# A causal convolution and a gated two-layer product on one core: channels in three chunks of 64, and the convolution a tile ahead

## The chip, the cores and the metric

The kernel runs on one core of a Trainium2 chip. The core has five engines with queues of their own: TensorE (PE in the profile, its weight loads PEld), VectorE (DVE), ScalarE (ACT), GpSimd (POOL) and SyncE (SP), whose queue issues most DMAs here. The metric is the device time of one execution, in microseconds (us); less is better.

## The reference

The input x has 8 sequences of 4096 tokens with 192 channels. Each of 8 heads (24 channels) has 7 weights, which a softmax turns into a causal filter over the tokens. The result, 32768 rows of 192, goes through a product with `w_in` (192 x 2048), the function h cos(h), and a product with `w_out` (2048 x 192).

```python
out = np.einsum('hk,bskhg->bshg', softmax(weight), x_unf)   # 7 taps, causal, zeros ahead of a sequence
h = out.reshape(B * S, D) @ w_in
g = h * np.cos(h)
return (g @ w_out).astype(np.float32)
```

## The kernel before

Tokens go in 64 tiles of 512 (index `t`), two of them a unit of 1024 (index `u`). The 2048 columns of `w_in` go in 8 pairs of 128 (index `j`); the work for one tile and one pair is called a slot here. In slot (t, j) TensorE computes product 1 (h, two PSUM banks, one for each of the pair's two blocks i), ScalarE the sine of h + pi/2, VectorE their product g in bf16. In the same slot TensorE runs an eighth of product 2 of the tile before, `mm2(t - 1, j)`: 16 matmuls of 192 columns. So g of a tile is made in one tile's slots and used in those of the next, and in slot 7 ScalarE copies the finished output from PSUM to SBUF (`o_sb`), which a later DMA stores.

All these matmuls use half of TensorE's rows (64 of 128); one on the upper and one on the lower half run at the same time, as long as they write different PSUM banks. Where the halves change banks, a `Turn` orders them: the last matmuls before the change mark a no-operation on SP's queue, and the first ones after it wait for that.

```python
def mark(self, *insts):
    self.nop = nc.sync.nop()
```

The convolution multiplies the tokens of a unit by banded 128 x 128 matrices, heads 4c to 4c + 3 in `conv_part(u, c)`: 12 matmuls of 192 columns, two halves of six with a Turn between them; ScalarE casts the result to bf16 into `ct`. `double_unit` (GpSimd) copies the upper 64 channels beside themselves, since 192 = 128 + 64 and product 1 takes the 64 on either row half. `turn_unit` transposes ct to cT (channels on partitions) by a DMA from SP. All of unit u + 1 is prepared in the two tiles of unit u: part 0 in slot 0 of the even tile, part 1 in slot 0 of the odd one, and there doubling in slot 0 and the transpose in slot 3.

Product 1 of a slot (class `Hidden`) is six half-row matmuls of 512 columns. `first` puts the upper half on bank 0 and the lower on bank 1 (two pairs), `last` the lower on bank 0 and the upper on bank 1 (one pair), with a Turn between them and product 2 in between to pass its time. Tile 0 has no product 2 and uses `full`, with 128-row matmuls in part.

The PSUM has 8 banks: three buffers of two banks for h (`h_pool`, taken in turn by product 1 and by the convolution's parts), one of two for the output (`o_ps`). An h buffer is free again when VectorE has made its product (or ScalarE has cast a convolution part). Each engine works through its instructions in the order in which the code writes them (`manual_schedule`).

Of the kernel before, what the change touches and what calls it, by code (L numbers as in the profile page):

```python
# [16 lines left out]
def kernel(  # L17
# [8 lines left out]
    nc = tc.nc  # L26
# [15 lines left out]
    C2 = D - 128  # L42
# [63 lines left out]
    w1 = consts.tile([128, Dff], BF16)  # L106
    w2 = consts.tile([128, NP, 128], BF16)
# [36 lines left out]
    def conv_part(u, c):  # L144
# [4 lines left out]

        def mm(i, k, start=False):  # L150
# [4 lines left out]
                out=ps[:, i // 2, (i % 2) * UB * G : (i % 2 + 1) * UB * G].rearrange("p (n g) -> p n g", g=G),  # L155
                lhsT=band[rows, h, 128 if prev else 0 : 256 if prev else 128],
                rhs=xb[rows, 0 if prev else 1 : UB if prev else UB + 1, h * G : (h + 1) * G],
# [6 lines left out]
        mm(3, 2)  # L164
        turn = Turn()
        turn.mark(up, mm(3, 1))
# [6 lines left out]
        mm(3, 0)  # L173
        if c == 0:
            ct_tiles[u] = ct_pool.tile([128, UB, 256], BF16, name="ct")
        o = ct_tiles[u][:, :, 4 * c * G : (4 * c + 4) * G].rearrange("p n (b i g) -> p b i n g", b=2, i=2)
        for b in range(2):
            nc.scalar.copy(o[:, b], ps[:, b, 0 : 2 * UB * G].rearrange("p (i n g) -> p i n g", i=2, n=UB))  # L178
# [4 lines left out]
    def double_unit(u):  # L183
        ct = ct_tiles[u]
        nc.gpsimd.tensor_copy(out=ct[:, :, D:256], in_=ct[:, :, 128:D])  # L185

    def turn_unit(u):
        ct = ct_tiles.pop(u)
        t = cT_pool.tile([128, UB, 2, 128], BF16, name="cT")
        nc.sync.dma_start_transpose(out=t.rearrange("p n c k -> p (n c) k"), in_=ct.rearrange("p n k -> p (n k)"))  # L190
        cT[u] = t
        cT.pop(u - 2, None)

    def conv_unit(u):
        for c in range(2):
            list(conv_part(u, c))
        double_unit(u)
        turn_unit(u)

    cast_unit(0)  # L200
    nc.gpsimd.tensor_copy(out=w2, in_=w2_f)  # L201
    nc.vector.tensor_copy(out=w1, in_=w1_f)  # L202
    conv_unit(0)
# [8 lines left out]
    class Hidden:  # L212


        def __init__(self, t, j):
            self.t, self.j = t, j
            self.c = cT[t // TPU]
            self.n0 = (t % TPU) * NB
            self.h = h_pool.tile([128, 2, T], FP32, name="h")

        def part(self, i, rows, w, c, start=False, stop=False):
            return nc.tensor.matmul(out=self.h[:, i, :], lhsT=w, rhs=self.c[rows, self.n0 : self.n0 + NB, c, :],  # L222
                             start=start, stop=stop)

        def w1(self, i, rows):
            f = 2 * self.j + i
            return w1[rows, f * 128 : (f + 1) * 128]

        def full(self):
            for i in range(2):  # L230
                r = slice(64 * i, 64 * i + 64)
                self.part(i, r, w2[r, self.j, :], 1, start=True)
            for i in range(2):
                self.part(i, slice(0, 128), self.w1(i, slice(0, 128)), 0, stop=True)

        def first(self):

            up, lo = slice(0, 64), slice(64, 128)
            self.part(0, up, self.w1(0, up), 0, start=True)
# [118 lines left out]
```

## Time and profile before

| | |
|---|---|
| median of 3 runs | 891.72 us (890.39 to 892.23) |
| the profiled execution | 885.45 us, its span from first to last instruction 883.7 us |
| busy in the span: TensorE, VectorE, ScalarE, GpSimd | 85%, 71%, 70%, 9% |
| mean granted clock of TensorE | 0.996 of full speed |
| starts of the output copies of tiles 1 and 63 | 57.67 and 872.33 us |

The profile is of one execution. Busy time is the time in which an engine has an instruction under way; on TensorE matmuls overlap, so their own durations add up to more than they cost. How long a piece of work takes TensorE is read from the distance of starts.

### The profile page before, as it was taken

The numbers are of one execution on the slowest core, as the hardware profiler recorded it, in microseconds if no ns is written. First come the engines' busy times: TensorE is split into PE (matmuls) and PEld (weight loads), VectorE is DVE, ScalarE is ACT, GpSimd is POOL, SyncE is SP. The second block draws the span as 40 slices with busy tenths as digits, with TensorE's granted clock in tenths as the row PEclk, the third lists the DMA queues.
The fourth block names the chain that finished last, engine by engine and source line by source line (L and its number), as shares of the span: only waits on it lengthen the run. The fifth ranks groups of instructions, "written<-read, shape, count | busy, mean of one in ns | idle before, by whom it ended". The sixth has DMA issues, their size and how long they took to land.

```text
span 883.7 us, 26935 instructions
## 1 busy us (share of the span) xinstructions
PE 751.2 (85%) x12016; PEld 535.3 (61%) x12016; DVE 631.0 (71%) x524; ACT 620.6 (70%) x707; POOL 76.3 (9%) x101
## 2 busy tenths in 40 slices
PE   0588989888889888889898898988888988889897
PEld 0166666666666566566666666666666665666665
DVE  1377777777777777777777777777777776767785
ACT  0477777777777777677777777777777766767775
POOL 1111110011111011110001111001111001110000
PEclk9999999999999999999999999999999999999999
DMA  8133332233332133332233332223333223332121
GB/s 238 24 79 80 98 88 71 55 97 89 87 97 72 46 94 94 83 97 72 49 93 93 83 97 74 70 70 98 79 96 94 58 62 97 80 96 73 44 61 56
DMA packets 138084, 72.52 MB, mean 82 GB/s; under 512 B 68200, under 2 KB 137840, under 8 KB 137840
## 3 DMA queue, kind: packets, MB, share of 16 engines
q1 hardware_dynamic: 136896, 70.27, 29.9%
q8 instruction: 94, 1.54, 0.7%
q10 hardware_dynamic: 1072, 0.53, 0.2%
q14 instruction: 22, 0.18, 0.1%
HBM read 28.84 MB, written 25.17 MB: 61 GB/s over the span
## 4 chain that ended last, share of the span: by engine, by line
issue 82%; POOL 8%; PE 6%; DMA 2%; ACT 1%; DVE 1%; SPq 0%; POOLq 0%; ACTq 0%
POOL x_bf L138 5%; PE o_ps L274 3%; PE h L222 2%; POOL ct L185 2%; DMA skew<-row_d 1%; POOL x_bf L137 1%; DMA row_d<-row 1%; DVE g L255 1%; PE h L154 0%; SPq L190 0%; ACT o_sb L284 0%; ACT cs L252 0%; POOL x_bf L135 0%; DMA w_sb<-in_weight_dram 0%; ACT L90 0%
## 5 line engine op out<-in xcount | busy, mean ns | idle before, releaser
L255 DVE TENSOR_TENSOR g<-h,cs 128x1024 bf16<-128x1024 f32 x512 | 626.2, 1224 | 225.8 <-ACT cs L252 200.5
L252 ACT ACTIVATE cs<-h 128x1024 bf16<-128x1024 f32 x512 | 525.2, 1026 | 176.5 <-PE h L222 176.4
L222 PE MATMUL h<-cT,w 64*128 64x512 bf16 x3056 | 520.0, 378 | 76.6 <-SPq L118 42.7
L274 PE MATMUL o_ps<-wo,g 64*128 64x192 bf16 x8192 | 514.5, 243 | 2.1 <-ACT o_sb L284 1.8
L274 PEld LDWEIGHTS <-g 64*128 64x128 bf16 x8192 | 395.6, 94 | 145.6 <-SPq L118 10.1
L222 PEld LDWEIGHTS <-w 64*128 64x128 bf16 x3056 | 160.0, 94 | 105.0 <-issue 55.1
L154 PE MATMUL h<-x_bf,band 64*128 64x192 bf16 x768 | 66.1, 250 | 49.3 <-DVE g L255 28.8
L154 PEld LDWEIGHTS <-band 64*128 64x128 bf16 x768 | 39.3, 95 | 93.2 <-DVE g L255 29.0
L178 ACT CAST ct<-h 128x384 bf16<-128x384 f32 x128 | 55.0, 482 | 47.2 <-PE h L154 37.4
L185 POOL COPY ct<-ct 128x512 bf16<-128x512 bf16 x32 | 19.6, 614 | 672.4 <-ACT ct L178 672.4
L284 ACT COPY o_sb<-o_ps 128x768 f32<-128x768 f32 x64 | 51.1, 798 | 33.6 <-PE o_ps L274 33.6
L138 POOL CAST x_bf<-x_f 128x1536 bf16<-128x1536 f32 x32 | 46.9, 1466 | 86.4 <-DMA x_f<-in_x_dram 86.4
L104 DVE COPY band<-skew 128x2048 bf16<-128x2048 bf16 x1 | 0.7, 695 | 15.2 <-DMA skew<-row_d 15.2
L137 POOL COPY x_bf<-x_bf 128x192 bf16<-128x192 bf16 x24 | 8.3, 347 | 0.0
L90 ACT ACT_TABLE_LOAD x1 | 1.3, 1283 | 2.2 <-DMA w_sb<-in_weight_dram 2.2
L135 POOL MEMSET x_bf<- 128x192 bf16 x8 | 2.1, 257 | 0.3 <-POOLq L342 0.3
L206 DVE CAST wo<-wo_f 128x768 bf16<-128x768 f32 x4 | 2.0, 555 | 0.0
L201 POOL CAST w<-w_f 128x1024 bf16<-128x1024 f32 x1 | 1.0, 1040 | 4.2 <-DMA w_f<-in_moe_w_in_dram 4.2
L252 ACT ACT_TABLE_LOAD x1 | 1.3, 1283 | 0.0
L202 DVE CAST w<-w_f 128x2048 bf16<-128x2048 f32 x1 | 1.2, 1221 | 0.0
L92 DVE TENSOR_REDUCE wsum<-wexp 8x1 f32<-8x7 f32 x1 | 0.1, 148 | 1.3 <-ACT wexp L90 1.3
L85 DVE MEMSET row<- 8x256 uint32 x1 | 0.3, 272 | 0.8 <-PEq L342 0.8
(9 smaller groups left out, 1.4 us busy)
## 6 DMA issues: line engine op xcount, KB each, us to landing
x_f<-in_x_dram SPq DMA_DIRECT2D x32, 768.0 KB, 4.8
out_dram<-o_sb SPq DMA_DIRECT2D x64, 384.0 KB, 2.6
wo_f<-in_moe_w_out_dram SPq DMA_DIRECT2D x1, 1536.0 KB, 13.2
w_f<-in_moe_w_in_dram SPq DMA_DIRECT2D x1, 1024.0 KB, 7.7
w_f<-in_moe_w_in_dram SPq DMA_DIRECT2D x2, 256.0 KB, 8.4
skew<-row_d ACTq DMA_DIRECT2D x1, 512.0 KB, 9.3
cT<-ct SPq DMA_TRANSPOSE x32, 4.3
w_sb<-in_weight_dram ACTq DMA_DIRECT2D x1, 0.2 KB
```

Of the source, the lines that this page charges most:

```text
L135: nc.gpsimd.memset(xb[:, 0, :], 0.0)
L137: nc.gpsimd.tensor_copy(out=xb[:, 0, :], in_=bf[u - 1][:, UB, :])
L138: nc.gpsimd.tensor_copy(out=xb[:, 1 : UB + 1, :], in_=xt)
L154: return nc.tensor.matmul(out=ps[:, i // 2, (i % 2) * UB * G : (i % 2 + 1) * UB * G].rearrange("p (n g) -> p n g", g=G), lhsT=band[rows, h ...
L178: nc.scalar.copy(o[:, b], ps[:, b, 0 : 2 * UB * G].rearrange("p (i n g) -> p i n g", i=2, n=UB))
L185: nc.gpsimd.tensor_copy(out=ct[:, :, D:256], in_=ct[:, :, 128:D])
L206: nc.vector.tensor_copy(out=wo[:, 4 * q : 4 * q + 4, :], in_=wo_f[:, 4 * q : 4 * q + 4, :])
L222: return nc.tensor.matmul(out=self.h[:, i, :], lhsT=w, rhs=self.c[rows, self.n0 : self.n0 + NB, c, :], start=start, stop=stop)
L252: nc.scalar.activation(out=cs, in_=self.h, func=AF.Sin, bias=math.pi / 2.0, scale=1.0)
L255: nc.vector.tensor_tensor(out=g_tiles[self.t][:, 2 * self.j : 2 * self.j + 2, :], in0=self.h, in1=cs, op=ALU.mult)
L274: m = nc.tensor.matmul(out=ps[:, b, si * D : (si + 1) * D], lhsT=g[rows, f, s * 128 : (s + 1) * 128], rhs=wo[rows, f, :], start=(swap == 0 ...
L284: nc.scalar.copy(sb.rearrange("p (b s) d -> p b (s d)", b=2), ps[:, :, 0 : 2 * D])
```

## The change

The 192 channels are cut into three chunks of 64 (`NC = 3`), eight channels of every head in each (`R = 8`), and every chunk is doubled. The weights of product 1 are loaded in the same cut, block i of a pair on row half i. So a slot's product 1 is three pairs; the upper row half writes bank 0 and the lower one bank 1 all the time, and no Turn is needed. The six matmuls stand ahead of all 16 of product 2, and the sine and product are issued there.

Part 0 of a unit's convolution is computed a tile earlier, in the odd tile two units before; part 1 in the even tile of the unit before, with the doubling in slot 0 and the transpose in slot 4 of that tile. In slot 0 the first half of a convolution part now stands ahead of product 1, the second half behind it, and the two casts are issued behind the slot's sine. The cast of x stands in slot 4 and its load in slot 6 of even tiles. Of the start, unit 1's part 0 and unit 2's load now stand ahead of the loop.

```diff
-    w1_f = consts.tile([128, Dff], FP32)
-    w2_f = consts.tile([128, NP, 128], FP32)
-    w2_src = moe_w_in[128:D, :].rearrange("c (j t f) -> t c j f", t=2, f=128)
-    nc.sync.dma_start(out=w1_f, in_=moe_w_in[0:128, :])
-    for t in range(2):
-        nc.sync.dma_start(out=w2_f[t * 64 : t * 64 + 64, :, :], in_=w2_src[t])
+    w_f = consts.tile([128, NC, NP, 128], FP32)
+    w_src = moe_w_in.rearrange("(h k r) (j t f) -> k t h r j f", h=H, r=R, t=2, f=128)
+    for k in range(NC):
+        for t in range(2):
+            nc.sync.dma_start(out=w_f[64 * t : 64 * t + 64, k, :, :], in_=w_src[k, t])
...
+        pv = ps[:, :, 0 : UB * 2 * G].rearrange("p b (n k i r) -> p b i n k r", n=UB, k=NC, i=2)
...
-                out=ps[:, i // 2, (i % 2) * UB * G : (i % 2 + 1) * UB * G].rearrange("p (n g) -> p n g", g=G),
+                out=pv[:, i // 2, i % 2],
...
         mm(3, 0)
+        yield
         if c == 0:
-            ct_tiles[u] = ct_pool.tile([128, UB, 256], BF16, name="ct")
+            ct_tiles[u] = ct_pool.tile([128, UB, NC, 2, 64], BF16, name="ct")
...
-        nc.gpsimd.tensor_copy(out=ct[:, :, D:256], in_=ct[:, :, 128:D])
+        nc.gpsimd.tensor_copy(out=ct[:, :, :, 1, :], in_=ct[:, :, :, 0, :])
...
-        t = cT_pool.tile([128, UB, 2, 128], BF16, name="cT")
+        t = cT_pool.tile([128, UB, NC, 128], BF16, name="cT")
...
+    load_unit(2)
+    list(conv_part(1, 0))
...
+    def mm1(t, j):
+        c = cT[t // TPU]
+        n0 = (t % TPU) * NB
+        h = h_pool.tile([128, 2, T], FP32, name="h")
+        for k in range(NC):
             for i in range(2):
...
+                rows = slice(64 * i, 64 * i + 64)
+                nc.tensor.matmul(out=h[:, i, :], lhsT=w[rows, k, j, :], rhs=c[rows, n0 : n0 + NB, k, :],
+                                 start=(k == 0), stop=(k == NC - 1))
+        cs = cos_pool.tile([128, 2, T], BF16, name="cs")
+        nc.scalar.activation(out=cs, in_=h, func=AF.Sin, bias=math.pi / 2.0, scale=1.0)
...
+        nc.vector.tensor_tensor(out=g_tiles[t][:, 2 * j : 2 * j + 2, :], in0=h, in1=cs, op=ALU.mult)
...
     for t in range(NT + 1):
-        u_next = t // TPU + 1
+        u, second = divmod(t, TPU)
+        cu, cc = (u + 2, 0) if second else (u + 1, 1)
         for j in range(NP):
...
+            conv = conv_part(cu, cc) if j == 0 and cu < NU else iter(())
+            next(conv, None)
+            if t < NT:
+                mm1(t, j)
+            next(conv, None)
+            next(conv, None)
+            if t > 0:
                 mm2(t - 1, j, 0, 8)
...
+            if j == 0 and second == 0 and cu < NU:
+                double_unit(cu)
+            if j == 4 and second == 0 and cu < NU:
+                turn_unit(cu)
+            if j == 4 and second == 0 and u + 2 < NU:
+                cast_unit(u + 2)
+            if j == 6 and second == 0 and u + 3 < NU:
+                load_unit(u + 3)
```

What this does to the order is shown at three places. The lines of the changed kernel are: L156 the convolution's matmul (before L154), L182 its cast (L178), L225 product 1 (L222), L228 the sine (L252), L249 product 2 (L274), L259 the output copy (L284). A number behind a name tells buffers apart, and `waits` names the engine whose semaphore an instruction waits for.

TensorE in an ordinary slot of tile 3 before, from the last pair of product 1 of one slot (h_871) to product 2 of the next (h_901):

```order
L222 LDWEIGHTS w1_120 [waits SP_sequencer_49]
L222 MATMUL h_871<-cT_384,w1_120 128x512
...
L274 LDWEIGHTS g_543
L274 MATMUL o_ps_761<-wo_122,g_543 128x192
...
L222 LDWEIGHTS w1_120
L222 MATMUL h_901<-cT_384,w1_120 128x512 [waits DVE_49]
...
L222 LDWEIGHTS w2_121
L222 MATMUL h_901<-cT_384,w2_121 128x512
...
L274 LDWEIGHTS g_543
L274 MATMUL o_ps_761<-wo_122,g_543 128x192
```

And now, from the end of one slot's product 2 to the product 2 behind the next slot's product 1:

```order
L249 LDWEIGHTS g_543
L249 MATMUL o_ps_792<-wo_123,g_543 128x192
L225 LDWEIGHTS w_122
L225 MATMUL h_890<-cT_259,w_122 128x512 [waits DVE_49]
...
L225 LDWEIGHTS w_122
L225 MATMUL h_890<-cT_259,w_122 128x512
...
L249 LDWEIGHTS g_543
L249 MATMUL o_ps_792<-wo_123,g_543 128x192
```

The six matmuls of product 1 (six weight loads, six matmuls; the first and the last shown) stand together, and the wait for SP's queue within product 1 is gone.

TensorE in slot 0 of tile 4 before: `first` of product 1 (h_983), the convolution's first half (h_989), `last`, the second half, product 2:

```order
L222 LDWEIGHTS w1_120 [waits DMAHW7_49]
L222 MATMUL h_983<-cT_869,w1_120 128x512 [waits DVE_49]
...
L154 LDWEIGHTS band_118 [waits DVE_49]
L154 MATMUL h_989<-x_bf_898,band_118 128x192 [waits Pool_49]
...
L222 LDWEIGHTS w1_120 [waits SP_sequencer_49]
L222 MATMUL h_983<-cT_869,w1_120 128x512
...
L154 LDWEIGHTS band_118 [waits SP_sequencer_49]
L154 MATMUL h_989<-x_bf_898,band_118 128x192
...
L274 LDWEIGHTS g_781
L274 MATMUL o_ps_1008<-wo_122,g_781 128x192 [waits Activation_49]
```

And now the convolution's first half (h_995), product 1 (h_1003), the second half, product 2:

```order
L156 LDWEIGHTS band_120
L156 MATMUL h_995<-x_bf_680,band_120 128x24x8 [waits DVE_49]
...
L225 LDWEIGHTS w_122 [waits DMAHW1_49]
L225 MATMUL h_1003<-cT_678,w_122 128x512 [waits DVE_49]
...
L156 LDWEIGHTS band_120 [waits SP_sequencer_49]
L156 MATMUL h_995<-x_bf_680,band_120 128x24x8
...
L249 LDWEIGHTS g_781
L249 MATMUL o_ps_1022<-wo_123,g_781 128x192 [waits Activation_49]
```

The convolution takes its h buffer ahead of product 1 of slot 0 instead of behind it, and product 1 is one piece between its halves.

ScalarE around the end of tile 1 before: the sine of slot 6, the output copy, the sine of slot 7, the casts of a convolution part, the sines of slots 0 and 1 of tile 2:

```order
L252 ACTIVATE cs_467<-h_443 128x1024 [waits DVE_49,PE_49]
L284 COPY o_sb_278<-o_ps_277 128x768 [waits PE_49]
L252 ACTIVATE cs_495<-h_470 128x1024 [waits DVE_49]
L178 CAST ct_520<-h_504 128x2x8x24 [waits DMAHW1_49,PE_49,Pool_49]
L178 CAST ct_520<-h_504 128x2x8x24
L252 ACTIVATE cs_541<-h_498 128x1024 [waits DVE_49]
L252 ACTIVATE cs_569<-h_545 128x1024 [waits DVE_49,PE_49]
```

And now, at the end of the same tile: the sine of slot 7, the output copy, the sine of slot 0, the casts, the sine of slot 1:

```order
L228 ACTIVATE cs_506<-h_499 128x1024 [waits DVE_49,PE_49]
L259 COPY o_sb_325<-o_ps_324 128x768 [waits PE_49]
L228 ACTIVATE cs_541<-h_534 128x1024 [waits DVE_49,PE_49]
L182 CAST ct_321<-h_526 128x24x16 [waits PE_49]
L182 CAST ct_321<-h_526 128x24x16
L228 ACTIVATE cs_579<-h_572 128x1024 [waits DVE_49,PE_49]
```

The sine of slot 7 stands ahead of the output copy and the sine of slot 0 ahead of the casts.

## Rows read from the trace of the kernel before

**Rows 1.** page, part 1: busy us (share) x instructions of each engine
```profile
PE 751.2 (85%) x12016; PEld 535.3 (61%) x12016; DVE 631.0 (71%) x524; ACT 620.6 (70%) x707; POOL 76.3 (9%) x101
```

**Rows 2.** page, part 5: groups | busy us, mean ns | idle before
```profile
L255 DVE TENSOR_TENSOR g<-h,cs 128x1024 bf16<-128x1024 f32 x512 | 626.2, 1224 | 225.8 <-ACT cs L252 200.5
...
L222 PE MATMUL h<-cT,w 64*128 64x512 bf16 x3056 | 520.0, 378 | 76.6 <-SPq L118 42.7
L274 PE MATMUL o_ps<-wo,g 64*128 64x192 bf16 x8192 | 514.5, 243 | 2.1 <-ACT o_sb L284 1.8
...
L154 PE MATMUL h<-x_bf,band 64*128 64x192 bf16 x768 | 66.1, 250 | 49.3 <-DVE g L255 28.8
```

**Rows 3.** timeline, one ordinary slot: start us, us, engine, line, operation, xcount [idle]
```profile
405.80 0.61 PE L222 MATMUL h<-cT,w 64*128 64x512 bf16 x4
...
406.23 0.68 PE L274 MATMUL o_ps<-wo,g 64*128 64x192 bf16 x12
...
406.72 0.40 PE L222 MATMUL h<-cT,w 64*128 64x512 bf16 x2
...
406.94 0.35 PE L274 MATMUL o_ps<-wo,g 64*128 64x192 bf16 x4
...
407.10 0.61 PE L222 MATMUL h<-cT,w 64*128 64x512 bf16 x4
407.15 1.02 ACT L252 ACTIVATE cs<-h 128x1024 bf16<-128x1024 f32 x1 [0.28 <-PE h L222]
```

**Rows 4.** timeline, the boundary from tile 28 to tile 29
```profile
412.33 0.61 PE L222 MATMUL h<-cT,w 64*128 64x512 bf16 x4
412.55 0.80 ACT L284 COPY o_sb<-o_ps 128x768 f32<-128x768 f32 x1 [0.45 <-PE o_ps L274]
...
413.24 1.03 ACT L252 ACTIVATE cs<-h 128x1024 bf16<-128x1024 f32 x1
413.41 0.34 PE L154 MATMUL h<-x_bf,band 64*128 64x192 bf16 x4 [0.47 <-DVE g L255]
...
414.31 1.23 DVE L255 TENSOR_TENSOR g<-h,cs 128x1024 bf16<-128x1024 f32 x1 [0.95 <-ACT cs L252]
414.56 0.86 ACT L178 CAST ct<-h 128x384 bf16<-128x384 f32 x2 [0.28 <-PE h L154]
...
415.58 0.61 PE L222 MATMUL h<-cT,w 64*128 64x512 bf16 x4 [0.41 <-DVE g L255]
```

**Rows 5.** timeline of ScalarE: output copies of tiles 1, 2, 61 and 63
```profile
57.67 0.80 ACT L284 COPY o_sb<-o_ps 128x768 f32<-128x768 f32 x1 [0.45 <-PE o_ps L274]
...
70.07 0.80 ACT L284 COPY o_sb<-o_ps 128x768 f32<-128x768 f32 x1 [0.45 <-PE o_ps L274]
...
850.14 0.80 ACT L284 COPY o_sb<-o_ps 128x768 f32<-128x768 f32 x1 [0.45 <-PE o_ps L274]
...
872.33 0.80 ACT L284 COPY o_sb<-o_ps 128x768 f32<-128x768 f32 x1 [0.45 <-PE o_ps L274]
```

**Rows 6.** timeline, the issue of a transpose on SP's queue, in an odd tile
```profile
419.85 1.72 SPq L190 DMA_TRANSPOSE cT<-ct  x1
...
421.68 0.39 PE L222 MATMUL h<-cT,w 64*128 64x512 bf16 x2 [1.07 <-SPq L118]
```

**Rows 7.** view of tile ct: durations ns min/median/max, last row us to landing
```profile
L185 POOL COPY ct<-ct x32: 613/614/615, 24.6 to 839.3; 128x512 bf16<-128x512 bf16 x32
L190 SPq DMA_TRANSPOSE cT<-ct x32: 1327/1920/3107, 25.2 to 843.8; - x32
...
DMA to landing us min/median/max: 4.3/4.3/5.0
```

**Rows 8.** timeline of the start: first product 1, first sines
```profile
29.67 1.58 PE L222 MATMUL h<-cT,w 64*128 64x512 bf16 x4 [6.06 <-DMA cT<-ct]
...
35.12 2.86 ACT L252 ACTIVATE cs<-h 128x1024 bf16<-128x1024 f32 x3
```

**Rows 9.** timeline of ScalarE: the last output copy
```profile
879.32 0.80 ACT L284 COPY o_sb<-o_ps 128x768 f32<-128x768 f32 x1 [5.27 <-PE o_ps L274]
```

More of the change, by code (lines that the diff above doesn't have):

```diff
@@ L41 @@
     NP = NF // 2
-    C2 = D - 128
+    NC = D // 64
+    R = G // NC
     xf = x.rearrange("b s d -> (b s) d")
@@ L104 @@
     nc.vector.tensor_copy(out=band, in_=skew[:, :, ::-1])
-    w1 = consts.tile([128, Dff], BF16)
-    w2 = consts.tile([128, NP, 128], BF16)
+    w = consts.tile([128, NC, NP, 128], BF16)
     wo = consts.tile([128, NF, D], BF16)
@@ L163, in conv_part @@
         mm(2, 2)
-        mm(3, 2)
+        mm(3, 1)
         turn = Turn()
-        turn.mark(up, mm(3, 1))
+        turn.mark(up, mm(3, 2))
         yield
@@ L210 @@
     o_state = {}
[L212 to L229, printed above, removed]
-            for i in range(2):
[L231 to L239, printed above, removed]
-            self.part(1, lo, self.w1(1, lo), 0, start=True)
-            self.turn = Turn()
-            self.turn.mark(self.part(0, up, w2[up, self.j, :], 1), self.part(1, lo, w2[lo, self.j, :], 1))
-        def last(self):
-            up, lo = slice(0, 64), slice(64, 128)
-            self.turn.wait(self.part(1, up, self.w1(1, up), 0, stop=True),
-                           self.part(0, lo, self.w1(0, lo), 0, stop=True))
-        def out(self):
-            cs = cos_pool.tile([128, 2, T], BF16, name="cs")
-            nc.scalar.activation(out=cs, in_=self.h, func=AF.Sin, bias=math.pi / 2.0, scale=1.0)
-            if self.j == 0:
-                g_tiles[self.t] = gpool.tile([128, NF, T], BF16, name="g")
-            nc.vector.tensor_tensor(out=g_tiles[self.t][:, 2 * self.j : 2 * self.j + 2, :], in0=self.h, in1=cs,
-                                    op=ALU.mult)
@@ L290 @@
     for t in range(NT + 1):
-        u_next = t // TPU + 1
+        u, second = divmod(t, TPU)
+        cu, cc = (u + 2, 0) if second else (u + 1, 1)
         for j in range(NP):
-            hid = Hidden(t, j) if t < NT else None
-            conv = conv_part(u_next, t % TPU) if j == 0 and t < NT and u_next < NU else None
-            if t == 0:
-                hid.full()
-                if conv:
-                    list(conv)
-            elif hid is None:
-                mm2(t - 1, j, 0, 8)
-            else:
-                hid.first()
-                if conv:
-                    next(conv)
-                    hid.last()
-                    next(conv)
-                    mm2(t - 1, j, 0, 8)
-                else:
-                    mm2(t - 1, j, 0, 6)
-                    hid.last()
-                    mm2(t - 1, j, 6, 8)
-            if hid is not None:
-                hid.out()
+            conv = conv_part(cu, cc) if j == 0 and cu < NU else iter(())
[5 more added lines that the diff above has]
+            if t > 0:
+                mm2(t - 1, j, 0, 8)
             if j == 2 and t > 1:
                 store(t - 2)
-            if t % TPU == TPU - 1 and u_next < NU:
-                if j == 0:
-                    double_unit(u_next)
-                if j == 3:
-                    turn_unit(u_next)
-                if u_next + 1 < NU:
-                    if j == 0:
-                        load_unit(u_next + 1)
-                    if j == 4:
-                        cast_unit(u_next + 1)
+            if j == 0 and second == 0 and cu < NU:
[6 more added lines that the diff above has]
+                load_unit(u + 3)
     store(NT - 1)
```

27 lines of the change are left out of this document (15 added, 12 removed).

## The prediction, made before the changed kernel ran

> **What bounds the kernel now.** I read the busy shares first: TensorE 85%, VectorE 71%, ScalarE 70% of a span of 883.7 us [rows 1]. None is full, so the question is which of them sets the pace where, and what it waits for. The groups by line give the work: 512 products on VectorE of 1.22 us, 8192 matmuls of 192 columns and 3056 of 512 columns [rows 2]. A matmul's mean there (243 and 378 ns) is no price: two run at once on the two row halves, and each is pipelined behind the one before it. The price is read from the timeline of an ordinary slot (one tile, one pair of d_ff blocks) as distances between starts [rows 3]: 4 matmuls of product 1, two pairs, take 406.23 - 405.80 = 0.43 us, so 0.215 a pair; 12 of product 2, six pairs, take 406.72 - 406.23 = 0.49, so 0.082 a pair. The slot is 407.10 - 405.80 = 1.30 us, and 3 x 0.215 + 8 x 0.082 = 1.30: TensorE never waits there. VectorE needs 1.22 of these 1.30 and ScalarE 1.02, so both follow. An ordinary slot is bound by TensorE, with the other two close behind.
>
> The tile's rhythm is read from the starts of the output copy, one a tile [rows 5]. Tile 2 comes 70.07 - 57.67 = 12.40 us after tile 1. Tiles 2 to 61 take 850.14 - 57.67 = 792.47; if the 30 even ones are all like tile 2, the 30 odd ones average (792.47 - 372.0) / 30 = 14.02. Tiles 62 and 63, without a convolution, take (872.33 - 850.14) / 2 = 11.10. The work of TensorE in a tile with a convolution part is 8 x 1.30 plus 6 pairs of 0.082, so 10.93. So 1.47 us are lost in each even tile, and 1.62 more in each odd one.
>
> Where the 1.47 goes stands in the timeline of a tile's boundary [rows 4]. Slot 0 starts at 412.33, and its first four matmuls run. The convolution stands next in TensorE's order and wants the h buffer of slot 6; VectorE frees it late, and it starts at 413.41. VectorE is late because ScalarE runs the output copy first (from 412.55, after the last product 2 of slot 7, 0.22 after the slot's end) and the sine of slot 7 only at 413.24; in an ordinary slot the sine starts 0.43 after the last matmul of product 1 has started [rows 3]. Then ScalarE copies the convolution (two casts, 0.86 from 414.56) before the sine of slot 0, and slot 1 starts at 415.58, where VectorE has just let go of slot 7's buffer (414.31 + 1.23, + 0.04).
>
> Where the 1.62 goes stands around the transpose [rows 6]. SP issues it for 1.72 us from 419.85, and the no-operations by which TensorE's row halves change banks wait on the same SP queue behind it: product 1 goes on at 421.68, with TensorE idle for 1.07 of it.
>
> **The change, part by part.** *Product 1.* Three chunks of 64 channels make 3 pairs a slot as before, upper half always into bank 0, lower half always into bank 1: 0.645 us, no change. The handover between its banks goes, 8 a tile; those of the convolution and of product 2 remain. All six matmuls now stand ahead of product 2, so the third pair starts at 0.43 of the slot instead of 0.92 (406.72 - 405.80), and by the same 0.43 of drain the sine starts at 0.86 instead of 1.35 after the slot's start. Each h buffer comes free half a microsecond sooner.
>
> *The transpose* now stands on SP behind product 2's handover and ahead of a load; the next handover on SP is that of the following tile's slot 0, some 5 us on. Issuing took 1.92 us in the median and 3.11 at most for 16 blocks [rows 7]; by the count of blocks that is 2.9 and 4.7 for 24, still hidden. The 1.62 goes.
>
> *Slot 0*, walked through with 0 at the start of slot 7's product 1, 0.04 for a semaphore between ScalarE, VectorE and TensorE [rows 4], and the durations above. The sine of slot 7 runs from 0.86 to 1.88, its product on VectorE to 3.15, the product of slot 6 one slot sooner, to 1.84. The output copy waits for the sine and runs 1.88 to 2.68 (product 2 of slot 7 was ready at 1.30 + 0.22). The convolution's first half takes slot 5's buffer, long free, from 1.31 to 1.56. Product 1 of slot 0 wants that of slot 6: it starts at 1.88, **0.32 late**, and ends at 2.53. Second half to 2.78, product 2 to 3.44; its o_ps is free at 2.72, just in time. The sine of slot 0 runs 2.74 to 3.76, VectorE 3.80 to 5.03. The casts now follow it, 3.76 to 4.62. Slot 1 starts at 3.44 (slot 7's buffer is free at 3.19); its sine has to let the casts pass, 4.50 to 5.52, VectorE to 6.79. Slot 2 starts at 4.75, where the casts have freed the convolution's buffer (4.66); slot 3 at 6.05 needs slot 0's (5.07), slot 4 at 7.36 needs slot 1's (6.83). Nothing waits, and slot 7 of the next tile starts at 3.44 + 6 x 1.305 = 11.27. The tile is 11.27 instead of 12.40 and 14.02. Without a convolution (tiles 61 to 63) product 2 of slot 0 waits for the copy until 2.72, and the tile is 2.72 + 0.66 + 7.83 = 11.21.
>
> *Doubling and transposing.* GpSimd doubles all 192 channels, 1536 values a partition instead of 512 in 0.61 us: between 0.61 and three times that, 1.84, and I take 1.84. The transpose lands after 4.3 us now [rows 7]; by its blocks 6.5, between 4.3 and 7.5 (1.5 x the slowest, 5.0). It is issued at about 7.6 on the clock above and wanted two tiles after slot 0, at 1.31 + 2 x 11.27 = 23.9: at 15.1 at the latest it is there. Cost nothing; the cover is 8.8 us.
>
> *The convolution's output* is laid out with runs of 8 words and gaps of 8, which no row of before shows; all its matmuls write without gaps. It reads in runs of 24 values and yet takes 250 ns where product 2 takes 243 [rows 2], which speaks for a price near zero. The other bound is that the pairs no longer run side by side, twice 0.49 us. Then the first half ends at 1.80, still hidden by the wait to 1.88, and the second adds 0.25 a tile, 61 x 0.25 = 15 us. I take zero, nearest to the row. The casts keep their 384 values each, and I keep 0.43 for one.
>
> *Start and end.* The first transpose comes 1.2 (doubling) + 2.2 (blocks) later than the one that released TensorE at 29.67 [rows 8]. Against that, unit 1's first part and the activation table are now done in its shadow, where the first sine stood 5.45 us behind (35.12); with product 1 at about 1.6 us as at 29.67 it would stand at 33.1 + 1.6 = 34.7, and the two casts behind it cost 0.9. I take +1, from 0 to +3, since six loads of weights in short rows stand in place of three. Tile 1 saves about 2.5, as an odd tile. At the end the copy of tile 63 to the last copy took 879.32 - 872.33 = 7.0 [rows 5, 9]; 2.72 + 64 x 0.082 + 0.22 - 1.88 = 6.3 now, so -0.7.
>
> **The sum.** From tile 1's copy to tile 63's: 59 x 11.27 + 3 x 11.21 = 698.5 instead of 872.33 - 57.67 = 814.66, so -116.2. With -2.5, -0.7 and +1 it is -118. The profiled execution took 885.45 in all, which gives 767. The median of the runs shown, 891.72, lies 6.3 above it; kept, that makes **774 us**.
>
> **The rivals.** *Gaps in PSUM cost.* The place and price stand above: +15, so 789; if a pair cost four times as much (1.97 a part), the first half would pass the wait by 0.41 and the second add 0.74, so 1.15 a tile, and 844. For it: no row shows such a write. Against: the runs of 24 that it reads cost nothing visible.
>
> The Trainium skill, PSUM — Partial Sum Buffer, section Specifications (TRN2), says that any non-contiguous pattern there slows matmuls significantly. No row of before shows that case; by this rule the time would be that of this rival, 789 or above, instead of 774.
>
> *Slot 0 keeps its loss.* The convolution still takes one of three h buffers, and ScalarE has the same three copies to place. If that cost 1.47 as now, only the handover would be won: 59 x 12.40 + 33.6 = 765.2, a gain of 49.5, with start and end about 841. Against it: product 1's result is ready 0.49 sooner, the output copy no longer stands before slot 7's sine, and the wait is for a buffer whose time is set by rows. It would take a sine or product that stays late by about 1.1 us from tile to tile, and ScalarE's 8 x 1.02 + 0.86 + 0.80 = 9.8 us leaves room in 11.27.
>
> *The transpose lands too late*, the rival on the slower side. Each unit's cT is wanted at the unit's slot 0, and TensorE stands in order behind it. It costs something once it lands more than 7.5 + 8.8 = 16 us after its issue, and the kernel is slower than before once it adds more than 118 / 31 = 3.8 us a unit to that, at 20 us. Only a stretch to more than four times the 4.3 us does that, and blocks are up by half; I expect about 900 there.
>
> **The numbers.** Forecast 70% (762 to 782), gaps 14% (783 to 800, a little of it far above), slot 0's loss 11% (about 841), the late transpose 3% (900), no change 2%. So faster by over 0.2%, which is about what a measurement of this kernel can tell from none, 95%; same 2%; slower 3%. The first two cases hold more than 8 in 10: 762 to 800.
>
> **What the profile will show.** If I am right, the output copies stand 11.2 to 11.3 us apart in odd and even tiles alike; TensorE has one idle stretch of some 0.3 us a tile, ahead of product 1 of slot 0 and released by VectorE; it never waits for SP while a transpose is issued; the sine starts 0.86 after a slot's start. The order on ScalarE at a tile's end is sine, output copy, sine, two casts. Convolution matmuls whose starts stand more than 0.08 a pair apart would show the gaps. Wrong I would be above all if ordinary slots came out longer than 1.30, since 504 of them multiply each 0.1 us to 50.

## The result, and the profile after

The changed kernel takes 774.44 us (774.11 to 775.25) against 891.06 of the kernel before in the same job; the ratio is 0.8693 with an interval of 0.8678 to 0.8708. Its profiled execution took 775.25, with a span of 773.5. The forecast was 774; how much of that is luck is told below.

The page of the changed kernel, parts 1 and 5, answers to [rows 1, 2] (L231 is the product on VectorE, L225 product 1, L156 the convolution):

```profile
PE 728.9 (94%) x12032; PEld 603.2 (78%) x12032; DVE 631.7 (82%) x524; ACT 613.4 (79%) x707; POOL 102.4 (13%) x101
...
L231 DVE TENSOR_TENSOR g<-h,cs 128x1024 bf16<-128x1024 f32 x512 | 626.1, 1224 | 105.9 <-ACT cs L228 77.0
...
L225 PE MATMUL h<-cT,w 64*128 64x512 bf16 x3072 | 494.0, 377 | 6.6 <-DVE g L231 2.3
...
L156 PE MATMUL h<-x_bf,band 64*128 64x192 bf16 x768 | 77.0, 250 | 30.7 <-DVE band L105 24.1
```

TensorE is busy for 94% instead of 85%, with nearly the same matmuls (product 1 has 3072 instead of 3056, since tile 0 now uses row halves as well). The idle time in front of product 1 fell from 76.6 to 6.6 us and no longer ends with SP's queue. The durations of single instructions are those of before.

The timeline of ScalarE, output copies of tiles 1 to 3, 62, 63 and the last one, answers to [rows 5, 9]:

```profile
58.28 0.79 ACT L259 COPY o_sb<-o_ps 128x768 f32<-128x768 f32 x1
...
69.65 0.79 ACT L259 COPY o_sb<-o_ps 128x768 f32<-128x768 f32 x1
...
81.01 0.79 ACT L259 COPY o_sb<-o_ps 128x768 f32<-128x768 f32 x1
```

The same view at the end:

```profile
751.21 0.79 ACT L259 COPY o_sb<-o_ps 128x768 f32<-128x768 f32 x1
...
762.34 0.79 ACT L259 COPY o_sb<-o_ps 128x768 f32<-128x768 f32 x1
768.95 0.80 ACT L259 COPY o_sb<-o_ps 128x768 f32<-128x768 f32 x1 [5.82 <-PE o_ps L249]
```

Odd and even tiles now take the same 11.36 to 11.37 us (69.65 - 58.28, 81.01 - 69.65), where they took 12.40 and 14.02 on average. From tile 1's copy to tile 63's it is 762.34 - 58.28 = 704.06 instead of 814.66: 110.6 us, where the two spans differ by 883.7 - 773.5 = 110.2: the gain lies in the loop.

The timeline at the boundary of two tiles, slot 7 and slot 0, answers to [rows 4]:

```profile
408.71 0.38 PE L225 MATMUL h<-cT,w 64*128 64x512 bf16 x1
...
409.74 1.02 ACT L228 ACTIVATE cs<-h 128x1024 bf16<-128x1024 f32 x1 [0.28 <-PE h L225]
...
410.02 0.24 PE L156 MATMUL h<-x_bf,band 64*128 64x192 bf16 x1
...
410.66 0.79 ACT L259 COPY o_sb<-o_ps 128x768 f32<-128x768 f32 x1
410.77 0.82 PE L225 MATMUL h<-cT,w 64*128 64x512 bf16 x6
...
411.63 1.02 ACT L228 ACTIVATE cs<-h 128x1024 bf16<-128x1024 f32 x1 [0.17 <-PE h L225]
...
412.24 0.38 PE L225 MATMUL h<-cT,w 64*128 64x512 bf16 x1
...
412.55 0.86 ACT L182 CAST ct<-h 128x384 bf16<-128x384 f32 x2
```

Slot 7's product 1 starts at 408.71, its sine at 409.74, ahead of the output copy at 410.66. Product 1 of slot 0 starts at 410.77, which is 2.06 after slot 7's; the prediction had 1.88. The idle stretch of 0.3 us a tile that it expected there does not show as idle time (VectorE ends only 2.3 us of it in all): the convolution's last matmuls are still under way, and the delay is read from the starts. The sine of slot 0 follows at 411.63, the casts only at 412.55, and slot 1 starts at 412.24 without a wait (before: at 415.58, 3.25 after slot 0's start).

The view of tile ct answers to [rows 7]:

```profile
L190 POOL COPY ct<-ct x32: 1467/1467/1467, 28.3 to 720.4; 128x1536 bf16<-128x1536 bf16 x32
L195 SPq DMA_TRANSPOSE cT<-ct x32: 3600/3647/4727, 29.8 to 723.7; - x32
...
DMA to landing us min/median/max: 7.4/7.4/7.4
```

The timeline while a transpose is issued, in an even tile:

```profile
405.30 3.63 SPq L195 DMA_TRANSPOSE cT<-ct  x1
405.44 0.84 PE L249 MATMUL o_ps<-wo,g 64*128 64x192 bf16 x14
405.82 1.02 ACT L228 ACTIVATE cs<-h 128x1024 bf16<-128x1024 f32 x1 [0.28 <-PE h L225]
...
406.10 0.38 PE L225 MATMUL h<-cT,w 64*128 64x512 bf16 x1
...
407.13 1.02 ACT L228 ACTIVATE cs<-h 128x1024 bf16<-128x1024 f32 x1 [0.28 <-PE h L225]
```

The landing in that view is that of one transpose alone, hence the three equal numbers. The issue holds SP's queue for 3.63 us, and TensorE and ScalarE go on in their rhythm of 1.31 meanwhile. The doubling takes 1.47 us.

### The profile page after: what moved, and what is told of

Its sections match the earlier page's. It is cut to its first block, busy times and chain, and to the rows that moved or that the text cites. A ratio compares the mean times of both kernels' runs of the same rounds, so it can differ in the third digit from the quotient of the medians.

```text
span 773.5 us, 26467 instructions
## 1 busy us (share of the span) xinstructions
PE 728.9 (94%) x12032; PEld 603.2 (78%) x12032; DVE 631.7 (82%) x524; ACT 613.4 (79%) x707; POOL 102.4 (13%) x101
## 4 chain that ended last, share of the span: by engine, by line
PE 75%; DVE 10%; ACT 9%; SPq 2%; DMA 2%; issue 1%; POOL 0%; ACTq 0%
PE h L225 38%; PE o_ps L249 34%; DVE g L231 10%; ACT cs L228 8%; DMA x_f<-in_x_dram 2%; PE h L156 2%; SPq L78 1%; ACT o_sb L259 1%; SPq L80 0%; ACT ct L182 0%; POOL x_bf L138 0%; ACT L228 0%; SPq L69 0%; SPq L195 0%; ACTq L228 0%
## 5 line engine op out<-in xcount | busy, mean ns | idle before, releaser
L231 DVE TENSOR_TENSOR g<-h,cs 128x1024 bf16<-128x1024 f32 x512 | 626.1, 1224 | 105.9 <-ACT cs L228 77.0
L228 ACT ACTIVATE cs<-h 128x1024 bf16<-128x1024 f32 x512 | 525.7, 1027 | 118.7 <-PE h L225 118.4
L249 PE MATMUL o_ps<-wo,g 64*128 64x192 bf16 x8192 | 507.8, 243 | 2.7 <-ACT o_sb L259 2.6
L225 PE MATMUL h<-cT,w 64*128 64x512 bf16 x3072 | 494.0, 377 | 6.6 <-DVE g L231 2.3
L249 PEld LDWEIGHTS <-g 64*128 64x128 bf16 x8192 | 451.3, 94 | 46.5 <-issue 3.9
L225 PEld LDWEIGHTS <-w 64*128 64x128 bf16 x3072 | 230.6, 94 | 71.0 <-issue 23.2
L190 POOL COPY ct<-ct 128x1536 bf16<-128x1536 bf16 x32 | 46.9, 1467 | 609.3 <-ACT ct L182 609.3
L156 PE MATMUL h<-x_bf,band 64*128 64x192 bf16 x768 | 77.0, 250 | 30.7 <-DVE band L105 24.1
L156 PEld LDWEIGHTS <-band 64*128 64x128 bf16 x768 | 56.0, 96 | 47.9 <-DVE band L105 24.0
L182 ACT CAST ct<-h 128x384 bf16<-128x384 f32 x128 | 54.9, 486 | 29.7 <-PE h L156 29.7
L259 ACT COPY o_sb<-o_ps 128x768 f32<-128x768 f32 x64 | 50.8, 793 | 5.8 <-PE o_ps L249 5.8
## 6 DMA issues: line engine op xcount, KB each, us to landing
skew<-row_d ACTq DMA_DIRECT2D x1, 512.0 KB, 12.4
```

What stands on the lines that cost most here:

```text
L156: return nc.tensor.matmul(out=pv[:, i // 2, i % 2], lhsT=band[rows, h, 128 if prev else 0 : 256 if prev else 128], rhs=xb[rows, 0 if prev ...
L182: nc.scalar.copy(ct_tiles[u][:, :, :, 0, w0 : w0 + 2 * R], ps[:, b, 0 : UB * 2 * G].rearrange("p (n k w) -> p n k w", n=UB, k=NC))
L190: nc.gpsimd.tensor_copy(out=ct[:, :, :, 1, :], in_=ct[:, :, :, 0, :])
L225: nc.tensor.matmul(out=h[:, i, :], lhsT=w[rows, k, j, :], rhs=c[rows, n0 : n0 + NB, k, :], start=(k == 0), stop=(k == NC - 1))
L228: nc.scalar.activation(out=cs, in_=h, func=AF.Sin, bias=math.pi / 2.0, scale=1.0)
L231: nc.vector.tensor_tensor(out=g_tiles[t][:, 2 * j : 2 * j + 2, :], in0=h, in1=cs, op=ALU.mult)
```

## The experiments

Each kernel was timed in three rounds beside the kernel before. Two readings stood against each other. By the first (A), the tile's loss is a wait for one of three h buffers, set by when the sine can run, plus the stall behind the transpose on SP's queue. By the other (B), what paid was something else: the handovers as such, or the convolution's new place. Where a run is about something else, its expectation says what A and B stand for. In the edits, `P1` is `mm1` cut in two: `part` gives the pairs of product 1, `out` the sine and the product.

**The third pair late again.** In slots 1 to 7 the changed kernel gets its third pair behind 12 matmuls of product 2:

```diff
+            split = 0 < t < NT and j > 0
             if t < NT:
-                mm1(t, j)
+                p = P1(t, j)
+                last = p.part(range(2) if split else range(NC))
+                if split:
+                    mm2(t - 1, j, 0, 6)
+                    p.part([2])
+                p.out()
...
-                mm2(t - 1, j, 0, 8)
+                mm2(t - 1, j, 6 if split else 0, 8)
```

> The changed kernel with the third pair of product 1 put back behind 12 of product 2's 16 matmuls in slots 1 to 7; no handover. Theory A (the tile's loss is the wait of slot 0 for slot 6's h buffer, so it grows by what the sine is later): the sine starts 0.49 us later in slot 6, the wait ahead of product 1 of slot 0 grows by 0.4 to 0.5, the tile goes from 11.37 to 11.8, the time from 774 to 799 to 806. Theory B (the gain came from the handovers that went, not from the earlier sine): tile 11.37, time 774 within 2.

Measured: 806.13 us (804.7 to 807.7), ratio 0.9031 (0.9017 to 0.9045). All tiles with a convolution take 11.86 or 11.87. In the timeline product 1 of slot 0 now shows a wait for VectorE:

```profile
404.02 0.82 PE L231 MATMUL h<-cT,w 64*128 64x512 bf16 x6 [0.57 <-DVE g L242]
```

The sine that comes half a microsecond later is paid for in full, once a tile: 0.50. A holds, with the time at the upper end of its range.

**ScalarE's order as before.** Sine and product of a slot are issued behind product 2 of the slot:

```diff
+            p = P1(t, j) if t < NT else None
+            if p:
+                p.part(range(NC))
...
             if t > 0:
                 mm2(t - 1, j, 0, 8)
+            if p:
+                p.out()
```

> The changed kernel with the sine and the product of a slot issued behind product 2 of the slot, as before: the output copy stands ahead of slot 7's sine and the two casts ahead of slot 0's. Theory A: slot 1 waits for slot 7's buffer, which comes free about 1.0 to 1.2 us later; the tile is 12.4 to 12.6, in odd and even tiles alike, the time 836 to 850. Theory B: the order on ScalarE is covered by its idle time, 774 to 780.

Measured: 837.02 us (836.69 to 837.48), ratio 0.9377 (0.9363 to 0.9391); every tile with a convolution 12.40. The boundary in its timeline:

```profile
405.99 0.80 ACT L270 COPY o_sb<-o_ps 128x768 f32<-128x768 f32 x1 [0.94 <-PE o_ps L260]
406.35 0.82 PE L231 MATMUL h<-cT,w 64*128 64x512 bf16 x6
...
406.68 1.03 ACT L239 ACTIVATE cs<-h 128x1024 bf16<-128x1024 f32 x1
...
407.60 0.87 ACT L182 CAST ct<-h 128x384 bf16<-128x384 f32 x2
...
409.02 0.82 PE L231 MATMUL h<-cT,w 64*128 64x512 bf16 x6 [0.85 <-DVE g L242]
```

The output copy (405.99) stands ahead of slot 7's sine (406.68), and slot 1 waits for slot 7's product, as in [rows 4] (0.85 us here; there 0.41, behind a wait of 0.47 ahead of the convolution). The tile is that of an even tile of before, to the hundredth. So the earlier third pair is worth nothing as long as ScalarE has the old order.

**ScalarE's order alone, on the kernel before.** Sine and product right behind product 1, all else as before:

```diff
                     hid.last()
+                    hid.out()
                     next(conv)
                     mm2(t - 1, j, 0, 8)
...
                     mm2(t - 1, j, 0, 6)
                     hid.last()
+                    hid.out()
                     mm2(t - 1, j, 6, 8)
-            if hid is not None:
-                hid.out()
```

> The kernel before with one part alone: the sine and product issued right behind product 1, so ahead of the output copy in slot 7 and of the two casts in slot 0; product 1, its handovers, the convolution's tile and the transpose as before. Theory A: slot 1 no longer waits for slot 7's buffer; even tiles 11.6 to 11.9 instead of 12.40, odd tiles shorter by the same 0.5 to 0.8, time 840 to 860. Theory B (the order on ScalarE is worth nothing without the earlier sine): 885 to 895.

Measured: 863.30 us (860.32 to 870.37), ratio 0.9680 (0.9634 to 0.9726). Even tiles 11.81, as A had it. The odd ones average 13.88, so that the stall behind the transpose grew from 1.62 to 2.07, which A had not foreseen: the time lies 3 us above its range. The trace shows where most of this comes from. Six of the 30 odd tiles took 15.5 to 16.0 us, and in each of these TensorE's wait for SP's queue is followed by a stretch at a granted clock of 0.50, the lower of its two levels; the other 24 stay at full clock, and in the kernel before one odd tile has such a stretch (16.5 us). One of the six in the timeline of TensorE:

```profile
305.88 0.39 PE L222 MATMUL h<-cT,w 64*128 64x512 bf16 x2 [2.05 <-SPq L118]
```

And the stretch behind it (busy time of TensorE, weight loads, VectorE, ScalarE, GpSimd, then the granted clock and the DMA share):

```profile
308.00:309.00 1.00, 1.00 (x10) 0.47 (x7) 0.59 (x1) 0.48 (x1) 0.00 (x0) 0.50 0.00 0
```

This tile, 21 by the output copies, took 15.7 us; tile 19, with a wait of 2.12 us and the full clock, took 14.1. At 1.6 us each the six cost some 10 us, an estimate, and without them the time would lie in A's range. The other 0.2 us of an odd tile's growth is a longer wait whose cause stays open.

These three and the two kernels make a table of tiles without the transpose's stall:

| | third pair late | third pair early |
|---|---|---|
| ScalarE's old order | 12.40 (before) | 12.40 |
| ScalarE's new order | 11.81 (on before), 11.87 (on after) | 11.37 (after) |

**The handover back.** The run with the third pair late, with a handover through SP in slots 1 to 7, though no bank is changed (the edit is against that run):

```diff
+                    turn = Turn()
+                    turn.mark(*last)
                     mm2(t - 1, j, 0, 6)
-                    p.part([2])
+                    turn.wait(*p.part([2]))
```

> The run with the late third pair, and with a handover through SP's queue in each of slots 1 to 7 as before (marked by the second pair, awaited by the third), though no bank is changed. Theory A: odd tiles as in that run (11.8), even tiles, in which SP issues the transpose for 3.6 us, longer by 2.5 to 3.5; the time is 75 to 110 us above that run's, near 890. Theory B: the handover costs in every slot, so odd tiles grow by 0.5 or more too.

Measured: 914.23 us (913.53 to 915.84), ratio 1.0244 (1.0229 to 1.0259): 108 us above the run without it, and slower than the kernel before. Odd tiles 11.73, no longer than without the handovers; even tiles 15.56 on average (14.14 to 16.38). The timeline of TensorE behind a transpose issued at 419.34:

```profile
420.15 0.82 PE L260 MATMUL o_ps<-wo,g 64*128 64x192 bf16 x12
423.13 0.39 PE L231 MATMUL h<-cT,w 64*128 64x512 bf16 x2 [2.16 <-SPq L118]
...
423.52 0.94 PE L231 MATMUL h<-cT,w 64*128 64x512 bf16 x4
424.26 1.17 PE L260 MATMUL o_ps<-wo,g 64*128 64x192 bf16 x12
425.22 0.64 PE L231 MATMUL h<-cT,w 64*128 64x512 bf16 x2
```

Stretches of the same place, with the columns named above:

```profile
412.90:419.30 6.40, 6.29 (x108) 5.52 (x109) 4.66 (x5) 5.30 (x8) 3.07 (x3) 1.00 0.20 64
...
424.00:425.00 1.00, 1.00 (x14) 0.72 (x10) 0.38 (x1) 0.59 (x1) 0.00 (x0) 0.50 0.24 46
425.00:426.00 1.00, 1.00 (x14) 0.71 (x12) 0.84 (x1) 0.11 (x1) 0.00 (x0) 0.50 0.42 56
```

A handover costs nothing in a slot; what costs is that it stands behind the transpose. TensorE is idle for 2.16 us here, and after that the granted clock is 0.50, the lower of the two levels, for the stretches to 427: product 2's 12 matmuls take 425.22 - 424.26 = 0.96 instead of 0.49. The 108 us lie in A's range for the difference (its "near 890" for the total was too low, since the run without handovers took 806), but A had only the wait in its sum, not the clock. The trace has such a stretch in 22 of the 30 even tiles. Tile 6, with a wait of 2.10 us, took 15.81 with it; tile 22, with a wait of 2.11, took 14.16 at full clock. At 1.65 us a tile some 36 of the 108 us are the clock's, an estimate; why it fell in the one tile and not in the other is not shown.

**The convolution behind product 1.** In slot 0 its first half follows two pairs of product 1 instead of standing ahead of it:

```diff
+            p = P1(t, j) if t < NT else None
+            if p:
+                p.part(range(2) if j == 0 and cu < NU else range(NC))
             next(conv, None)
-            if t < NT:
-                mm1(t, j)
+            if p:
+                if j == 0 and cu < NU:
+                    p.part([2])
+                p.out()
```

> The changed kernel with the convolution's first half behind two pairs of product 1 of slot 0 instead of ahead of it. Theory A: the wait for slot 6's buffer only moves, from product 1 to the convolution; tile 11.25 to 11.4, time 767 to 776. Theory B (the place ahead of product 1 is what won at the boundary): tile 11.8 to 12.4, time 800 to 840.

Measured: 771.03 us (770.52 to 772.58), ratio 0.8641 (0.8627 to 0.8656); tile 11.32. A holds: the place is not what won; the other one is even 0.05 us a tile better.

**The convolution's output without gaps.** The matmuls write PSUM head by head as before:

```diff
-                out=pv[:, i // 2, i % 2],
+                out=ps[:, i // 2, (i % 2) * UB * G : (i % 2 + 1) * UB * G].rearrange(
+                    "p (n k r) -> p n k r", n=UB, k=NC),
```

> The changed kernel with the convolution's matmuls writing PSUM without gaps, head by head, as before; the channels then stand in another order. Theory A (runs of 8 words cost nothing): 774 within 1.5, convolution matmuls 250 ns as now. Theory B (gaps slow a matmul): 5 to 20 us faster, the distance of the convolution's starts shorter.

Measured: 773.33 us (773.03 to 775.81), ratio 0.8660 (0.8644 to 0.8676); tile 11.37, the same as with gaps. In the groups by line:

```profile
L156 PE MATMUL h<-x_bf,band 64*128 64x192 bf16 x768 | 77.1, 250 | 30.6 <-DVE band L105 24.0 <-POOL x_bf L138 6.0 <-DVE g L232 0.3
```

250 ns a matmul with and without gaps. The ratio lies 0.4% below that of the changed kernel; the median is 1.1 us lower here, and that of the kernel before, timed anew in another job, 1.4 us higher. The loop does not differ.

**The convolution's halves balanced.** A count of the changed kernel's 12 matmuls shows 4 on the upper and 8 on the lower half (the taps on a block's second half and those on the block before both read the lower half). Here half of the matmuls on the block before go to the upper half:

```diff
-            rows = slice(0, 64) if k == 0 else slice(64, 128)
+            upper = k == 0 or (k == 2 and i % 2 == 1)
+            rows = slice(0, 64) if upper else slice(64, 128)
...
-        up = mm(1, 0)
+        mm(1, 0)
         mm(2, 2)
-        mm(3, 1)
+        up = mm(1, 2)
```

The order of the twelve matmuls changes with it (in part shown), and the two that moved read other tokens than the result needs.

> The changed kernel with half of the convolution's matmuls on the previous block moved from the lower to the upper row half, so that each half has 6 of 12 instead of 4 and 8 (for the heads concerned the tokens that the matmul reads are then the wrong ones). Theory A (the lower half lags by two matmuls of 192 columns, 0.17 us, behind each convolution, and with it the sine of slots 1 to 7): the sine starts 0.86 instead of 1.03 behind a slot's start, the tile is 11.20 to 11.30 instead of 11.37, time 764 to 770. Theory B (the two halves' load does not matter, the lag has another cause): 11.37, 774 within 1.5.

Measured: 768.76 us (767.73 to 769.51), ratio 0.8609 (0.8594 to 0.8624); tile 11.29. Its timeline of slot 7 and slot 0:

```profile
404.86 0.83 PE L226 MATMUL h<-cT,w 64*128 64x512 bf16 x6
...
405.72 1.02 ACT L229 ACTIVATE cs<-h 128x1024 bf16<-128x1024 f32 x1 [0.28 <-PE h L226]
...
406.17 0.43 PE L157 MATMUL h<-x_bf,band 64*128 64x192 bf16 x6
...
406.75 0.82 PE L226 MATMUL h<-cT,w 64*128 64x512 bf16 x6 [0.16 <-DVE g L232]
```

The sine starts 0.86 after the slot, as the prediction had it, and product 1 of slot 0 1.89 after slot 7's. In the changed kernel the lower half runs 0.17 behind the upper one through slots 1 to 7, and the sine with it.

**The start: weights behind the band.** The first convolution waits for the band matrices, which land at 23 us. Both weight loads wait for them here, behind a no-operation on SP's queue that waits for the band's transfer:

```diff
     load_unit(0)
...
-            nc.sync.dma_start(out=w_f[64 * t : 64 * t + 64, k, :, :], in_=w_src[k, t])
...
-    nc.sync.dma_start(out=wo_f, in_=moe_w_out.rearrange("(n p) d -> p n d", p=128))
     load_unit(1)
...
+    gate = nc.sync.nop()
...
+            nc.sync.dma_start(out=w_f[64 * t : 64 * t + 64, k, :, :], in_=w_src[k, t])
...
+    nc.sync.dma_start(out=wo_f, in_=moe_w_out.rearrange("(n p) d -> p n d", p=128))
```

> The changed kernel with the loads of both weight matrices issued only once the band matrices have landed, and the load of unit 1 ahead of them. Theory A (the first convolution waits for two small transfers that crawl behind 4.6 MB of bulk loads): the band lands at 10 to 15 us instead of 23, the first product 1 starts 5 to 11 us sooner, time 763 to 769. Theory B (the small transfers are slow by themselves): the band still lands near 20, the weights come later, time 774 to 785.

Measured: 775.81 us (774.48 to 776.27), ratio 0.8686 (0.8670 to 0.8702): no gain, and A fails on the time. The band landed at 12.0, as A had it, but the convolution's own handover then stood behind 8.45 us of weight issues on SP, and the first product 1 started at 34.92 instead of 35.61.

**The start: weights on ScalarE's queue.**

```diff
-            nc.sync.dma_start(out=w_f[64 * t : 64 * t + 64, k, :, :], in_=w_src[k, t])
+            nc.scalar.dma_start(out=w_f[64 * t : 64 * t + 64, k, :, :], in_=w_src[k, t])
```

> The changed kernel with the weights of product 1 loaded from ScalarE's queue behind the band's transfer, those of product 2 from SP's queue behind the handovers of unit 0's convolution, and unit 1's load ahead. Theory A (in the run with the weights behind the band the band landed in time, but the convolution's handover then stood on SP behind 8 us of weight issues): the band lands at 12 to 14 us, the first product 1 starts at 26 to 30 instead of 35.6, time 765 to 769. Theory B (the start is bound by the volume of the loads, not by a queue's order): first product 1 at 33 to 36, time 772 to 777.

Measured: 774.41 us (773.58 to 774.74), ratio 0.8673 (0.8656 to 0.8689). A fails; the time and the first product 1 lie where B had them. The start in its timeline:

```profile
12.24 0.69 DVE L103 COPY band<-skew 128x2048 bf16<-128x2048 bf16 x1 [7.85 <-DMA skew<-row_d]
...
13.00 3.29 PE L154 MATMUL h<-x_bf,band 64*128 64x192 bf16 x24 [13.00 <-DVE band L103]
...
22.44 10.21 SPq L193 DMA_TRANSPOSE cT<-ct  x1
...
33.39 1.46 PE L154 MATMUL h<-x_bf,band 64*128 64x192 bf16 x12 [8.40 <-SPq L116]
...
34.78 1.47 PE L224 MATMUL h<-cT,w 64*128 64x512 bf16 x6
```

The convolution starts at 13.0, the transpose is issued at 22.44, but this issue lasts 10.21 us instead of 3.7, and product 1 starts at 34.78. The view of tile ct has the landings of this run:

```profile
DMA to landing us min/median/max: 5.5/6.1/12.2
```

The longest is that of the first transpose: it lands at 22.44 + 12.2 = 34.64, and product 1 starts 0.14 us behind it. Whatever was moved ahead was given back there. TensorE also waits 8.40 us for SP's queue in front of the second half of unit 1's first part (33.39): at the start the changed kernel still has a handover behind a transpose, but here the landing ends later. That the volume of the loads is the cause, as B has it, is not shown.

**The convolution in slot 3.** Its halves stand around product 2, and from slot 3 on product 2 stands ahead of product 1:

```diff
+            conv_here = j == 3 and cu < NU
+            if t == 0 or j < 3:
...
+            else:
+                conv = conv_part(cu, cc) if conv_here else iter(())
+                next(conv, None)
                 mm2(t - 1, j, 0, 8)
+                next(conv, None)
+                next(conv, None)
+                if t < NT:
+                    mm1(t, j)
```

> The changed kernel with the convolution part in slot 3 instead of slot 0, its halves around product 2, and product 2 ahead of product 1 in slots 3 to 7 (the transpose in slot 6, the load in slot 7). Theory A (what is left of the tile's loss is the wait for an h buffer behind the convolution; 0.66 us of product 2 in that place cover it, and two products 1 in a row at the tile's end cover the output copy): tile 11.08 to 11.18, which is 8 x 1.306 plus 8 matmuls of 192 columns on the lower half, time 756 to 762. Theory B (the wait goes wherever the convolution goes): 11.3 to 11.5, time 770 to 780.

Measured: 771.98 us (771.29 to 772.83), ratio 0.8644 (0.8625 to 0.8663); tile 11.36, and 10.70 without a convolution. My number for A fails, and both lie in B's range. The timeline at a tile's boundary:

```profile
397.91 0.79 ACT L259 COPY o_sb<-o_ps 128x768 f32<-128x768 f32 x1
...
398.59 2.88 ACT L228 ACTIVATE cs<-h 128x1024 bf16<-128x1024 f32 x3
...
399.67 2.35 DVE L231 TENSOR_TENSOR g<-h,cs 128x1024 bf16<-128x1024 f32 x2 [0.39 <-ACT cs L228]
...
400.06 0.84 PE L249 MATMUL o_ps<-wo,g 64*128 64x192 bf16 x16
...
400.94 0.82 PE L225 MATMUL h<-cT,w 64*128 64x512 bf16 x6
```

The convolution costs its 8 matmuls of 0.082 here (11.36 - 10.70 = 0.66) and no wait. But in the new order the output copy (397.91) stands ahead of slot 7's sine (398.59) again, and slot 2's product 1, due at 400.06 + 8 x 0.082 = 400.72, starts at 400.94, just behind the end of slot 7's product (399.67 + 1.22 = 400.89). The tiles without a convolution have this wait as well (10.70, where 8 x 1.306 is 10.45), so it does not go where the convolution goes, as B has it. The mechanism is A's; the wait was made anew by my own order.

**All three together**, the halves balanced by a small transfer that copies a block's last 6 tokens to the upper partitions:

```diff
+    def tail_unit(u):
+        nc.sync.dma_start(out=xtail[u % 2][58:64, :, :], in_=bf[u][122:128, 0:UB, :])
```

> The changed kernel with the convolution in slot 3, the start's loads from ScalarE's queue, and half of the convolution's matmuls on the previous block on the upper row half, for which a small transfer copies that block's last 6 tokens to the upper partitions. Theory A: the three gains add up; tile 10.93 to 11.02, start 6 to 9 us sooner than now, time 738 to 750. Theory B (they overlap, or the small transfer holds SP's queue): 750 to 766.

Measured: 763.23 us (762.54 to 763.69), ratio 0.8548 (0.8532 to 0.8564), the fastest of all and clear of the changed kernel. Tile 11.20 = 10.70 + 0.50, the balanced convolution; of the start little was won (first product 1 at 33.9). A's sum fails, since the wait of the run before stays (10.70), and the time lies in B's range.

## Why the prediction was right, and where only by luck

**The walk through slot 0** was right in its mechanism. The two runs that undo one part of it each (third pair, ScalarE's order) cost 32 and 63 us and put the wait where the walk has it; the table shows that the new order by itself brings 0.53 to 0.59 of a tile's 1.03, and the earlier third pair nothing without it and 0.44 to 0.50 with it. Of the 110 us in the loop that makes 59 x 1.03 = 61 for slot 0, and 30 x 1.62 = 49 for the stall behind the transpose.

**The term that was mis-sized** is the sine's start, "at 0.86 instead of 1.35 after the slot's start": it is 1.03, since I counted the convolution as 6 pairs where it is 4 matmuls on one half and 8 on the other. By that count the work of a tile of before is 11.1 instead of 10.93, and its loss 1.3 instead of 1.47. Of 0.18 us in the wait of slot 0, 0.10 remain in the tile: 11.37, not 11.27. The balanced run gives 11.29, so this settles all but 0.02 of the term.

**The handovers**: "the 1.62 goes" was right, and of more weight than I gave it. With the third pair late, the same handover behind the 24-block transpose costs 108 us (914.23 against 806.13), about a third of it by the lower clock, an estimate. So the three chunks with a late third pair and its handover are slower than the kernel before (914 against 893).

**The transpose** stayed hidden. Its issue took 3.65 us (I had 2.9, at most 4.7), its landing 7.4 in the one that the view gives; in the run with the weights on ScalarE's queue it was 5.5 at least and 6.1 in the median (I had 6.5, at most 7.5; only that run's first, at 12.2, was longer). The doubling took 1.47, within my bounds of 0.61 and 1.84.

**The gaps in PSUM** cost nothing, as I took it. The Trainium skill, PSUM — Partial Sum Buffer, section Specifications (TRN2), says that any non-contiguous pattern slows matmuls significantly; for runs of 8 words with gaps of 8 these runs do not agree, 250 ns and a tile of 11.37 with gaps and without.

**Start and end.** I had tile 1's copy at 57.67 - 2.5 + 1 = 56.2; it came at 58.28, so the start cost 3.1 instead of 1, just above the bound of 3. The page has the band matrices' transfer landing 12.4 us after its issue instead of 9.3, and the first convolution starts at 24.05 instead of 20.31. The end took 768.95 - 762.34 = 6.6 instead of 6.3.

**The sum and the luck.** Against the predicted span of 765.4 the measured 773.5 is 8.1 more: 59 x 0.10 = 5.9 from the tiles, 2.1 from the start, 0.3 from the end, less 0.2 in the tiles without a convolution. I then added 6.3 because the median of before lay above its profiled execution; here the median lies 0.8 below it. The two errors, +8.1 and -7.1, cancel to within 1 us. Taken by itself the mechanism gave 767 and the chip 775, 1% apart.

What stays open: why the first product 1 starts at 34 to 36 us however the loads are ordered. The transpose's issue lasted 3.7, 5.6 and 10.2 us in three orders of the loads, longest where it was issued earliest; that it waits for the bulk loads under way fits, but no run took the loads away. Nor does any run put the convolution back into its old tile: that the doubling and the longer transpose need the earlier one is argued from their times.

## What to carry to other kernels

When a ring of a few buffers joins three engines, walk one boundary by hand with starts from the timeline: the gain came from when the sine could run, an earlier matmul was worth nothing until ScalarE's order let the sine follow it, and that order alone brought half. A semaphore handed on by a queue that also issues transfers waits behind their issue; look at what stands ahead of it there. Count the work of each row half of TensorE by itself, not in pairs, and do not add the offset between one profiled execution and a median to a forecast as if it were a constant.

## What the runs showed of the hardware that was not expected

A half of TensorE's rows that has more work lags behind the other for slots on end (0.17 us through slots 1 to 7, gone with a balanced convolution). Issuing a transpose of 24 blocks takes 3.65 us, one of 16 took 1.92 in the median; landing went from 4.3 in the median to 6.1 (17 of the 32 transposes of the run with the weights on ScalarE's queue, 5.5 to 7.4 but for the first), a little less than by the count of blocks. With bulk loads about, the issue alone took 10.2. In the run with the handover back, TensorE idle for 2.16 us was followed by stretches at a granted clock of 0.50, where the matmuls took twice as long, at a cost of some 1.65 us; after an equal wait in another tile the clock stayed at full. In the changed kernel, without such waits, the mean clock was 1.0.
